# The quarter sums of the output weights on another engine, and two hand-dealt orders dealt anew

## The chip, the cores and the metric

The kernel runs on one core of a Trainium2 chip, in one launch. The core has five engines with instruction queues of their own: TensorE (PE in the profile; its weight loads are listed as PEld), VectorE (DVE), ScalarE (ACT), GpSimd (POOL) and SyncE (SP), which here only issues transfers. Each engine runs its queue in order. The metric is the device time of an execution in microseconds; the kernel before took 757.24 us, the median of three runs (756.76 to 757.77).

## The reference

```python
# attention: x (8, 8, 512, 64), state (8, 8, 32, 64): batch, heads, tokens or states, width
scores  = x @ state.T / 8;   a  = softmax(scores);   xread = a  @ state
scores2 = state @ x.T / 8;   a2 = softmax(scores2);  sread = a2 @ x
y = concatenate([xread, sread], axis=2)          # 544 rows for each batch and head
# bridge: (B, H, S, D) -> (B*S, H*D): 4352 rows of 512
# feed forward: d_model 512, d_ff 1536
xn  = y / sqrt(mean(y*y) + 1e-6) * rms_g
out = (silu(xn @ w_gate) * (xn @ w_val)) @ w_out     # (4352, 512) fp32
```

The three weight matrices arrive as 64-bit floats and are turned into fp32 in the kernel.

## The kernel before

**Batches.** The eight batches are worked one after the other, and then the 256 state rows of all batches together. For each batch the tokens' part of the attention is folded into the weights: the scores' softmax is aT_s, and own_weights (L702, copied by ACT at L714) multiplies the state into the gate and value weights, so that hidden_seven (L849) computes gate and value as v x aT_s. Batches 1 to 7 save products in the manner of Strassen and Winograd, seven for eight, with sums made on DVE and POOL: more_of_v (POOL, L729 to L732) and slot_sums (POOL, L767 to L770) for the inputs, L912 and L925 (DVE) to gather results, where L925 frees the PSUM bank of a pair of row blocks for the pair after next.

**The output product.** project_twice (L1152) applies the seven-product scheme twice. The outer seven products, counted o = 0 to 6, use seven outer blocks of the output weights, listed by outer_weights(): four blocks of wo and the three sums of them, kept in wt, which weight_sums (DVE, L995) makes once. Each outer product consists of seven inner ones; three of them need quarter sums of the outer block (w2) and three need quarter sums of h (h2, DVE, L1200 to L1206). quarter_sums of h are made anew in each batch. Those of the weights are made once, in batch 1, by weight_quarters: four differences of 128x384 fp32 for each of the seven outer blocks, the first three into a tile w2, the fourth in place; then w2 (576 KB) is written to DRAM (t2_d, t_d in the profile, L1108). From then on every batch fetches the seven sets back, one after the other, through a pool of three buffers (fetch_quarters, L1098). The same pool holds the w2 tiles while the sums are made, so a sum or a fetch waits until the tile three allocations earlier is free: written out, or read by the last product that uses it.

**The batch's own sums.** The results of the outer products are added by DVE (L1192) and combined by POOL (combine, L1180 to L1185), then stored by SP. Meanwhile the attention of the next batch is computed in pieces: scores (L356), softmax steps on DVE (L424 to L443), reading (L449), the row norm (DVE L393 and L396, PE L399, POOL L300, PE L307), and the states' part (L643).

**What sets the order.** The order of all five queues is written out by hand: each part of the work is a generator, and a string names which generator takes its next step. ORDER covers the first stretch: batch 0 (hidden, L745; project_as_ready, L952), the attention of batches 0 and 1, the conversion of the weights (exponents on ACT, L247 to L253; values on DVE, L274 to L283), and the start of batch 1. FIRST covers batch 1, PERIOD batches 2 to 6, LAST batch 7, STATES the state rows. Letters that matter here: z is one filler product (keep_awake, L1287), whose result nobody reads; k in ORDER is one step of weight_sums; w starts batch 1; S is the states' part of batch 1's attention; q in FIRST is one step of weight_quarters; G and g are fetches of quarter sets; f is a fetch of w; p, h, t, u are steps of the products and sums. A step that issues a transfer puts it on SP's queue at that place, and SP waits there until the transfer may start.

```python
streams.update(q=weight_quarters(), G=first_fetches_of_quarters())
...
for stream in FIRST if b == 1 else LAST if b + 1 == B else PERIOD:
    next(streams[stream])
```

Of the kernel before, what the change touches and what calls it, by code (L numbers as in the profile page):

```python
# [14 lines left out]
ALU = mybir.AluOpType  # L15
# [7 lines left out]
FLAT = 1793.0  # L23

ORDER = (
    "zzzzaaaadzzzababadeebebadzbzaddzabaeebeesabaszadbeazzzzdaaazbbbzzzszdsdzeezabazb"
    "AzeAbeddAbezedabazaAbbaavdbsbsvvdAAazdeazzzeAzhdstzdddehedAuehtddzhzddveevdpeuAd"
    "veAehdddepdAtdpddAdeeeAAhddehAtdAdApeevAuhspdvAesdveuAeeAdespdAsdddhdAdtepshduph"
    "eepAddvdephevtdevheAdduedASSpsthhededudAAepseeehdedAtAvsupdApeddvvdhAdAAddephdAh"
    "ApdedAtutdAdevdhdAdveAAeSvhutAhAhShpStdukSwwSwwkwwuwkppSkkppwSkkScpSSkcskkpSpwks"  # L30
    "Scck"
)

PERIOD = (
# [4 lines left out]
)  # L39

FIRST = (
    "htqhhqvtaaaxthuaqhuxqvvhatqhqtquhqaqhtquhqhxaqxquhtxfuhutqhthuhhqauthhthxuqquauq"
    "uqhxhaxtttuahhutxhvxhhGxaqkkukxuhkuhtthaqatqhuhauasGhthuqsGuuhuhtfttuahuhhgahlut"
    "huuuuftapaupsuhupupugkaappckppkpscpppkkqkpkkppkpkkppppfpakkakckppapkkkpkcapskppp"
    "acappaaapcsaapkaskakaakgkqpqpqpppkaksppaqkkgppapkpaakppaposakspokasckoosgagwswxo"
    "sxowpsxxcfsxlooxgf"
)
LAST = (
    "vxhhffththhtuhhhavuttuuhhtfuhhgxxthhhuuuxxtuthuhtthuhuxhutuvxxxvhthhutkxghhtuhut"
# [11 lines left out]
def kernel(  # L61
# [21 lines left out]
    VE, SE, GE, TE = nc.vector, nc.scalar, nc.gpsimd, nc.tensor  # L83
# [47 lines left out]
    def load_x(b, *queues):  # L131
# [6 lines left out]
        for c in range(NC):  # L138
# [12 lines left out]
                     in0=ones.to_broadcast([P, NC]), op=ALU.pow)  # L151
# [6 lines left out]
    for i in range(4):  # L158
        GE.tensor_copy(groups[:, i], ident[:, 0:Ns])
        for j in range(1, 4):  # L160
            GE.tensor_tensor(out=groups[:, i], in0=groups[:, i],
                             in1=ident[:, Ns * j:Ns * j + Ns], op=ALU.add)
# [336 lines left out]
    def second_half():  # L499

        yield from chunk_scores(1)
        yield from half_read(1)
# [260 lines left out]
    def slot_sums(b):  # L763

        tt = aT_t[b] = seven["late"].tile([P, 3, HS], F32, name="aT_t")
        b11, b12, b21, b22 = (aT_s[b][:, e, HS * i:HS * i + HS] for e in range(2) for i in range(2))
        GE.tensor_tensor(out=tt[:, 0], in0=b12, in1=b11, op=ALU.subtract)  # L767
        GE.tensor_tensor(out=tt[:, 1], in0=b22, in1=tt[:, 0], op=ALU.subtract)
        GE.tensor_tensor(out=tt[:, 2], in0=b21, in1=tt[:, 1], op=ALU.subtract)
        GE.tensor_tensor(out=b12, in0=b22, in1=b12, op=ALU.subtract)  # L770
# [14 lines left out]
    def tokens_of(b):  # L785

        return ([[aT_s[b][:, e, HS * i:HS * i + HS]] for e in range(2) for i in range(2)],
                [[aT_t[b][:, i]] for i in range(3)])
# [196 lines left out]
    def weight_sums():  # L985

        t1, t2, t4 = (seven["t"][:, i] for i in range(3))
        for k in range(0, HM, 2):
            def blk(i, j):
                return wo[:, HM * i + k:HM * i + k + 2, HD * j:HD * j + HD]  # L990
            for dst, a, b in ((t1[:, k:k + 2], blk(0, 1), blk(0, 0)),
                              (t2[:, k:k + 2], blk(1, 1), t1[:, k:k + 2]),
                              (blk(0, 1), blk(1, 1), blk(0, 1)),
                              (t4[:, k:k + 2], blk(1, 0), t2[:, k:k + 2])):
                VE.tensor_tensor(out=dst, in0=a, in1=b, op=ALU.subtract)  # L995
                yield
# [89 lines left out]
    def outer_weights():  # L1086

        t = seven["t"]

        def blk(i, j):  # L1090
            return wo[:, HM * i:HM * i + HM, HD * j:HD * j + HD]
        return [blk(0, 0), blk(1, 0), t[:, 1], t[:, 0], blk(0, 1), blk(1, 1), t[:, 2]]

    def fetch_quarters(n):

        if n < 7 * (B - 1):
            w2_sb[n] = seven["w2"].tile([P, 3, QM, QD], F32, name="w2")
            nc.sync.dma_start(out=w2_sb[n], in_=t2_d[n % 7])  # L1098

    def weight_quarters():  # L1100

        for o, (b11, b21, b12, b22) in enumerate(map(by_columns, outer_weights())):
            w2 = seven["w2"].tile([P, 3, QM, QD], F32, name="w2")
            for to, a, b in ((w2[:, 0], b12, b11), (w2[:, 1], b22, w2[:, 0]),
                             (w2[:, 2], b21, w2[:, 1]), (b12, b22, b12)):
                GE.tensor_tensor(out=to, in0=a, in1=b, op=ALU.subtract)  # L1106
                if to is b12:
                    nc.sync.dma_start(out=t2_d[o], in_=w2)  # L1108
                yield

    def by_columns(r):

        return [r[:, QM * i:QM * i + QM, QD * j:QD * j + QD] for j in range(2) for i in range(2)]
# [130 lines left out]
    def first_fetches_of_quarters():  # L1244

        for n in range(3):
            fetch_quarters(n)
            yield
# [25 lines left out]
    def of_batch_0(part):  # L1274

        for m in range(NM):
            if m not in parts_0:
                parts_0[m] = hidden(m, lambda e, k, m=m: v_sb[0, m // 2][0][:, e, m % 2, k, :],
                                    [aT_s[0][:, e, :] for e in range(2)])
            yield from parts_0[m][part]  # L1280

    def keep_awake():


        ps = fz.tile([P, 2, P], F32, name="f")
        while True:
            TE.matmul(out=ps, lhsT=ident, rhs=ident.unsqueeze(1).to_broadcast([P, 2, P]),  # L1287
                      start=True, stop=True)
            yield

    def first_of_batch(b):
        slot_sums(b)
        yield
        for mp in range(2):
            for part in own_weights(b, mp):
                yield from part
# [19 lines left out]
    for k in range(2, RAW_AHEAD):  # L1316
# [3 lines left out]
    streams = {"a": first_half(), "b": second_half(), "s": states_read(0), "A": tokens_read(1), "S": states_read(1),  # L1320
               "e": exponents(), "d": values(),
               "v": (step for mp in range(NM // 2) for part in own_weights(0, mp) for step in part),
               "h": of_batch_0(0), "t": of_batch_0(1), "u": of_batch_0(2),
               "p": project_as_ready(banks_0), "c": projected(banks_0, store_tokens(0)),
               "w": first_of_batch(1), "k": weight_sums(), "z": keep_awake()}
    by_hand = dict(engines={mybir.EngineType.PE, mybir.EngineType.DVE,
                            mybir.EngineType.Activation, mybir.EngineType.Pool,
                            mybir.EngineType.SP})
    with tc.manual_schedule(**by_hand):
        for stream in ORDER:  # L1330
            if stream in "ckw" and "s" not in seven:
                early.close()
                open_late()
            next(streams[stream])
        assert all(next(stream, done) is done for name, stream in streams.items() if name != "z")

        for b in range(1, B):
            h, t, u = hidden_seven(S, weights_of(b), lambda b=b: tokens_of(b), True)
            p, c, k, o = project_twice(b, store_tokens(b))
            own = [own_weights(b, mp) for mp in range(2, NM // 2)]  # L1340
            then = [own_weights(b + 1, mp) for mp in range(2)] if b + 1 < B else []
            streams = {"h": h, "t": t, "u": u, "p": p, "c": c, "k": k,
                       "v": (step for part in own for step in part[0]),
                       "x": (step for part in own + then for step in part[1])}
            streams.update(o=o, f=fetches(b), g=fetches_of_quarters(b))
            if b == 1:
                streams.update(q=weight_quarters(), G=first_fetches_of_quarters())
            if b + 1 < B:
                streams.update(l=loads(b + 2) if b + 2 < B else iter((0, 0)), a=tokens_read(b + 1), s=states_read(b + 1),
                               w=first_products(b + 1, then))  # L1350
            else:
                streams["a"] = (step for part in (state_norm(), sums_of_w([0])) for step in part)
            for stream in FIRST if b == 1 else LAST if b + 1 == B else PERIOD:
                next(streams[stream])
            assert all(next(stream, done) is done for stream in streams.values())
        n = B * (NM // 2)
        h, t, u = hidden_seven(NT, (state_weights, state_sums), state_tokens, True,
                               lambda mp: fetch(n + mp + W_BUFS))
        p, c, k = project_seven(NT, store_states, nc.scalar)
        list(weights_back())  # L1360
        streams = {"h": h, "t": t, "u": u, "p": p, "c": c, "k": k, "y": sums_of_w(range(1, NM // 2))}
        for stream in STATES:
            next(streams[stream])
        assert all(next(stream, done) is done for stream in streams.values())
# [29 lines left out]
```

## Time and profile before

| | |
|---|---|
| runs | 757.77, 757.24, 756.76 us |
| profiled execution, its own time | 756.69 us |
| its span, first to last instruction | 754.9 us |
| mean granted clock of TensorE | 0.998 |
| DRAM read, written | 116.46 MB, 28.77 MB |
| quarter sums on POOL (L1106) | 28, from 124.9 to 198.7 us |
| writes of the sets (L1108), fetches (L1098) | 7 and 49 of 576 KB |

Times within the profile are microseconds from the span's start. Busy times are those of one engine; a line number such as L1152 is the line of the kernel before. An fp32 product is listed as two passes, so the counts of matmul records are twice those of the instructions. In lists in order of time, the bracket behind a row says how long the engine had been idle before it and what ended that. The granted clock is the share of full speed that TensorE was given.

### The profile page before, as it was taken

How to read it: one execution, taken by the hardware profiler on the slowest of the kernel's cores; microseconds unless marked ns; L12 is line 12 of the kernel's file. 1: busy time of each engine (PE TensorE's matmuls, PEld its weight loads, DVE VectorE, ACT ScalarE, POOL GpSimd, SP SyncE). 2: the span in 40 equal slices, each digit the busy share in tenths (PEclk: the TensorE clock that was granted, in tenths of full speed). 3: DMA queues.
4: the chain of work that ended last, by engine and by line, in shares of the span. 5: the costliest groups of instructions: out<-in, count | busy, mean ns of one | idle time of the engine just before them, and what ended most of it. 6: DMA issues, size and time to landing. Idle time of an engine off the chain costs nothing.

```text
span 754.9 us, 14333 instructions
## 1 busy us (share of the span) xinstructions
PE 747.0 (99%) x5636; PEld 601.0 (80%) x5636; DVE 581.8 (77%) x982; ACT 350.2 (46%) x547; POOL 296.9 (39%) x387
## 2 busy tenths in 40 slices
PE   9999999999999999999999999999999999999998
PEld 7744444779868898879877997799788987899997
DVE  4897774789937996689858994799579965787952
ACT  6899863553244622653255415542456236411220
POOL 3000017971484227532565128312842275324600
PEclk9999999999999999999999999999999999999999
DMA  9998734934876077626673477527661855132411
GB/s 293 275 338 301 265 150 145 353 117 158 299 232 232 17 305 237 239 56 231 229 274 105 154 264 244 176 81 294 215 224 22 307 203 216 54 115 97 140 56 29
DMA packets 60995, 146.16 MB, mean 194 GB/s; under 512 B 14848, under 2 KB 31744, under 8 KB 54016
## 3 DMA queue, kind: packets, MB, share of 16 engines
q1 hardware_dynamic: 47808, 125.78, 47.1%
q10 hardware_dynamic: 13120, 19.47, 8.9%
q8 instruction: 45, 0.74, 0.4%
q14 instruction: 22, 0.18, 0.1%
HBM read 116.46 MB, written 28.77 MB: 192 GB/s over the span
## 4 chain that ended last, share of the span: by engine, by line
PE 96%; DMA 2%; DVE 1%; POOL 1%; issue 0%; ACT 0%; SPq 0%; POOLq 0%
PE f L849 39%; PE f L1152 29%; PE f L952 6%; PE pv L745 6%; PE at L702 3%; PE pv L702 3%; PE f L1015 2%; PE f L1287 2%; DMA t_d<-w 1%; PE at L643 1%; PE at L356 1%; DMA w<-t_d 1%; PE at L449 1%; PE pv L516 0%; PE at L307 0%; POOL w L1106 0%
## 5 line engine op out<-in xcount | busy, mean ns | idle before, releaser
L849 PE MATMUL f<-aT_s,v 128*128 128x256 f32 x504 | 119.6, 382 | 0.0
L849 PEld LDWEIGHTS f<-aT_s,v 128*128 128x128 f32 x504 | 94.5, 190 | 25.2 <-issue 11.4
L1180 POOL TENSOR_TENSOR kept<-kept 128x256 f32<-128x256 f32 x28 | 23.1, 826 | 189.7 <-DVE kept L1192 188.6
L1165 ACT COPY kept<-f 128x512 f32<-128x512 f32 (+1 forms) x56 | 29.7, 531 | 140.2 <-PE f L1152 98.4
L849 PE MATMUL f<-aT_t,vs 128*128 128x256 f32 x336 | 87.0, 382 | 0.0
L912 DVE TENSOR_TENSOR g<-g,f 128x512 f32<-128x512 f32 x84 | 57.4, 686 | 37.6 <-PE f L849 31.4
L1152 PE MATMUL f<-w,h 128*128 128x128 f32 x588 | 75.4, 278 | 0.0
L1152 PEld LDWEIGHTS f<-w,h 128*128 128x128 f32 x588 | 70.7, 194 | 4.9 <-issue 4.9
L849 PEld LDWEIGHTS f<-aT_t,vs 128*128 128x128 f32 x336 | 62.8, 190 | 14.0 <-POOL vs L729 3.7
L903 ACT ACTIVATE hb<-g 128x1024 f32<-128x1024 f32 x42 | 44.4, 1057 | 54.1 <-DVE g L912 54.1
L729 POOL TENSOR_TENSOR vs<-v 128x256 f32<-128x256 f32 x42 | 31.3, 745 | 80.7 <-ACT v L714 80.6
L300 POOL TENSOR_TENSOR ri<-ss,mhalf 128x4 f32<-128x4 f32 (+1 forms) x9 | 11.1, 1236 | 107.9 <-DVE s L603 78.6
L901 ACT COPY g<-f 128x512 f32<-128x512 f32 x42 | 24.6, 586 | 44.8 <-PE f L849 44.8
L952 PE MATMUL f<-wo,hb 128*128 128x512 f32 x96 | 45.2, 599 | 0.0
L745 PE MATMUL pv<-aT_s,v 128*128 128x512 f32 x96 | 44.4, 597 | 0.0
L849 PE MATMUL f<-aT_s,vs 128*128 128x256 f32 x168 | 43.6, 382 | 0.0
L849 PE MATMUL f<-aT_t,v 128*128 128x256 f32 x168 | 43.4, 381 | 0.0
L1152 PE MATMUL f<-wo,h 128*128 128x128 f32 x336 | 42.4, 276 | 0.0
L925 DVE TENSOR_TENSOR hb<-hb,f 128x512 f32<-128x512 f32 (+1 forms) x48 | 31.0, 647 | 14.8 <-PE f L849 14.8
L1152 PE MATMUL f<-wo,hb 128*128 128x128 f32 x336 | 42.1, 275 | 0.0
L912 DVE TENSOR_TENSOR c<-c,f 128x512 f32<-128x512 f32 (+1 forms) x48 | 31.3, 651 | 13.6 <-PE f L849 13.6
L925 DVE TENSOR_TENSOR hb<-hb,c 128x512 f32<-128x512 f32 (+1 forms) x48 | 36.7, 765 | 6.1 <-ACT hb L903 5.3
(225 smaller groups left out, 1680.7 us busy)
## 6 DMA issues: line engine op xcount, KB each, us to landing
w_m<-w_d SPq DMA_DIRECT2D x48, 1024.0 KB
w<-t_d SPq DMA_DIRECT2D x49, 576.0 KB
out_dram<-kept SPq DMA_DIRECT2D x28, 256.0 KB
raw<-in_moe_w_val_dram SPq DMA_DIRECT2D x6, 1024.0 KB
raw<-in_moe_w_out_dram SPq DMA_DIRECT2D x6, 1024.0 KB
w_d<-w_m SPq DMA_DIRECT2D x6, 1024.0 KB
x_b<-in_x_dram SPq DMA_DIRECT2D x6, 1024.0 KB
x_d<-xB ACTq DMA_DIRECT2D x6, 1024.0 KB
```

The costliest lines, as they stand in the source:

```text
L702: TE.matmul(out=pv[e][Ns * j:Ns * j + Ns, :], lhsT=stT_g[b][D * e:D * e + D, j, :], rhs=w[D * e:D * e + D, j].rearrange("p m k f -> p (m k ...
L729: GE.tensor_tensor(out=vs[:, 0], in0=a21, in1=a22, op=ALU.add)
L745: TE.matmul(out=to[0], lhsT=lhs(i, k), rhs=r, start=(i == 0), stop=(i == len(rhs) - 1))
L849: TE.matmul(out=ps[:, i, 0:half], lhsT=l[:, i, :], rhs=r, start=(start and i == 0 and k == 0), stop=(k == len(lhs) - 1), skip_group_check= ...
L901: SE.copy(gates(q)[1], q["x"][:, :, 0:half])
L903: SE.activation(out=hb[:, 2 * mp:2 * mp + 2, 0:n].rearrange("p m (c t) -> p m c t", c=2), in_=q["g"][:, :, :, 0:half], func=ACTF.Silu if s ...
L912: VE.tensor_tensor(out=to, in0=to, in1=q[ps][:, :, 0:half], op=ALU.add)
L925: VE.tensor_tensor(out=part, in0=part, in1=val, op=ALU.mult)
L952: TE.matmul(out=banks[r], lhsT=hb[:, m, P * r:P * r + P], rhs=wo[:, m, :], start=(m == 0), stop=(m == NM - 1))
L1152: TE.matmul(out=to[half][:, slot, :], lhsT=lhs[:, k, :], rhs=rhs[:, k, :], start=(fresh and n in (0, 4) and k == 0), stop=(k == QM - 1), s ...
L1165: SE.copy(of_half(k, i), banks[name][i])
L1180: GE.tensor_tensor(out=k[:, 4:8:3], in0=k[:, 5:6].to_broadcast([P, 2, QD]), in1=k[:, 4:8:3], op=ALU.add)
```

## The change

weight_quarters gets the engine and the list of outer blocks as arguments. The sums of blocks 2, 3 and 6, which are the three in wt, are made by VectorE at the end of the first stretch (twelve letters Q in ORDER); those of blocks 0, 1, 4 and 5, which lie in wo, are made by VectorE in batch 1 (sixteen q in FIRST, 28 before). GpSimd makes none. Each set is still written to DRAM by SP behind its fourth sum, and fetched as before, except that in the new FIRST the fetch of block 3 stands ahead of that of block 2. ORDER has 416 letters (404 before): the same letters and the twelve Q, in a new order. FIRST has 326 (338 before): the same letters and twelve q fewer, in a new order. PERIOD, LAST and STATES are untouched. From the inserted line on, line numbers are one higher.

```diff
 ORDER = (
-    "zzzzaaaadzzzababadeebebadzbzaddzabaeebeesabaszadbeazzzzdaaazbbbzzzszdsdzeezabazb"
...
-    "ApdedAtutdAdevdhdAdveAAeSvhutAhAhShpStdukSwwSwwkwwuwkppSkkppwSkkScpSSkcskkpSpwks"
-    "Scck"
+    "zzzzzzaaaaazzbbadedabdebezzaadazbbzezeaezbbsabadzzdbsbdzzabazabadszeeazbezdbbzza"
...
+    "dSdAeSAAhheApdAtAdASheuvAtvdevdhuhdShhSShtSwtkkuwuskSpkSkkpQpsppwkkkkpQpQQccQwpc"
+    "QQkkQQwwQwwSQQwc"
 )
...
 FIRST = (
-    "htqhhqvtaaaxthuaqhuxqvvhatqhqtquhqaqhtquhqhxaqxquhtxfuhutqhthuhhqauthhthxuqquauq"
...
-    "sxowpsxxcfsxlooxgf"
+    "vqahtaqaahhathhthhqxhuuuxthaqatvquvxthxqxqhtquhuuhhhutqhfqttuaaqxhhhtquqqaaxuhxh"
...
+    "cofxox"
 )
...
-    def weight_quarters():
-
-        for o, (b11, b21, b12, b22) in enumerate(map(by_columns, outer_weights())):
+    def weight_quarters(engine, *outer):
+
+        for o in outer:
+            b11, b21, b12, b22 = by_columns(outer_weights()[o])
             w2 = seven["w2"].tile([P, 3, QM, QD], F32, name="w2")
             for to, a, b in ((w2[:, 0], b12, b11), (w2[:, 1], b22, w2[:, 0]),
                              (w2[:, 2], b21, w2[:, 1]), (b12, b22, b12)):
-                GE.tensor_tensor(out=to, in0=a, in1=b, op=ALU.subtract)
+                engine.tensor_tensor(out=to, in0=a, in1=b, op=ALU.subtract)
                 if to is b12:
                     nc.sync.dma_start(out=t2_d[o], in_=w2)
                 yield
...
-               "w": first_of_batch(1), "k": weight_sums(), "z": keep_awake()}
+               "w": first_of_batch(1), "k": weight_sums(), "Q": weight_quarters(VE, 2, 3, 6), "z": keep_awake()}
...
-                streams.update(q=weight_quarters(), G=first_fetches_of_quarters())
+                streams.update(q=weight_quarters(VE, 0, 1, 4, 5), G=first_fetches_of_quarters())
```

## The prediction, made before the run

> **What bounds the kernel now.** I read the busy shares first, then who TensorE (PE) waits for, then the stretches, then the chain that ended last and the order of time around the one hole.
>
> ```profile
> PE 747.0 (99%) x5636; PEld 601.0 (80%) x5636; DVE 581.8 (77%) x982; ACT 350.2 (46%) x547; POOL 296.9 (39%) x387
> ...
> PE f L1287 <- POOL ident masks.py:199: 1.7, 1, 1.7
> PE f L1152 <- DMA w<-t_d: 1.1, 1, 1.1
> PE at L399 <- DVE part L396: 0.9, 1, 0.9
> PE f L849 <- DVE hb L925: 0.5, 1, 0.5
> ```
>
> PE is busy for 99% of the span and has four named waits. So the span is PE's work plus its holes, and the change adds or removes no matmul: both orders hold 34 filler matmuls (L1287) and the same products. All it can win lies in holes, and in what they do to PE's clock.
>
> ```profile
> 33.00:132.00 99.00, 99.00 (x502) 43.28 (x501) 74.14 (x100) 76.74 (x97) 16.86 (x20) 1.00 0.67 240
> 132.88:217.59 84.71, 82.65 (x670) 69.77 (x675) 71.30 (x119) 33.89 (x57) 50.47 (x54) 0.98 0.66 226
> 217.59:297.91 80.32, 80.32 (x671) 68.31 (x678) 65.02 (x116) 34.78 (x58) 35.11 (x47) 1.00 0.58 198
> 208.50:213.00 4.50, 4.49 (x25) 4.49 (x26) 2.11 (x5) 0.59 (x1) 3.80 (x5) 0.62 0.87 302
> ```
>
> Columns: stretch, its length, busy time of PE, weight load, VectorE (DVE), ScalarE (ACT) and GpSimd (POOL), granted PE clock, DMA share, GB/s. The first stretch has no hole from 33 to 132 us: nothing to win there. Batch 1 (second row) takes 84.71 us and batch 2, the same stream without quarter sums, 80.32: batch 1 loses 4.39. The last row is 4.5 us in which the clock was 0.62.
>
> ```profile
> 201.95 1.50 PE L1152 MATMUL f<-w,h 128*128 128x128 f32 x12
> 203.28 1.50 PE L1152 MATMUL f<-wo,h 128*128 128x128 f32 x12
> 204.62 1.50 PE L1152 MATMUL f<-wt,hb 128*128 128x128 f32 x12
> 207.00 0.36 PE L399 MATMUL at<-part,groups 128*128 128x16 f32 x2 [0.88 <-DVE part L396]
> 208.51 1.65 PE L1152 MATMUL f<-w,hb 128*128 128x128 f32 x6 [1.14 <-DMA w<-t_d]
> 209.95 2.45 PE L1152 MATMUL f<-w,h 128*128 128x128 f32 x12
> 212.24 0.83 PE L1152 MATMUL f<-wt,h 128*128 128x128 f32 x6
> ...
> 188.22 7.04 DMA t_d<-w
> 195.34 1.01 POOL w L1106
> 196.42 1.02 POOL w L1106
> 197.50 1.21 POOL w L1106
> 198.73 3.23 DMA t_d<-w
> 202.01 6.45 DMA w<-t_d
> ```
>
> The lower lines are the chain that ended last. POOL's sums of the seventh set wait for a buffer until set 5 has been written to DRAM (7.04), then are made, written (3.23) and fetched back (6.45); PE needs them at 208.5.
>
> **What is removed.** Waits: 0.88 + 1.14 = 2.02 us. Slow clock: the x6 and x12 after the hole take 1.44 and 2.29 from start to start (208.51, 209.95, 212.24), where the same shapes took 0.67 and 1.33 at 201.28 and 201.95: 0.77 + 0.96 = 1.73. Together 3.75. The clock row says the same: 4.5 x (1 - 0.62) = 1.71. Of the 4.39 the other 0.64 has no named cause, so the gain lies between 3.75 and 4.39; I take 3.75.
>
> Here a rule of the Trainium skill (TensorE: Matmul & The Clock Gate, "Why this matters for your kernels") reads otherwise: the clock falls only after idle gaps of over about 3 us. The row differs, since no gap here exceeds 1.14 and the granted clock behind it is 0.62. By the rule the removed wait would be worth 2.02 alone; the row decides.
>
> Both waits go. The DMA wait: in the changed order set 5, the last, is summed among the first four quarter sums of h (the first, L1200, began at 156.99), so by about 159 us, and all seven writes stand on SP's queue ahead of the first fetch; set 6 is needed at 208. The L396 wait: DVE stands one 384-element sum earlier (0.47) when it reaches L396, and DVE operations between 195 and 200 that POOL's sums stretched (L1204 0.81, L1206 1.35, L1200 1.35, against 0.55) fall back: 1.9. Together 2.4 against the 0.88.
>
> **What is added on DVE.** 28 sums of 128x384, off POOL. POOL took 1.0 to 1.3 each (medians by form). On DVE the same shape with two SBUF operands is L1200 to L1206: 0.55 busy, 0.47 apart when POOL is idle (183.37, 183.84), up to 1.34 beside POOL (156.99). I take 0.5, since with its sums POOL loses about half of its 50.5 us in batch 1 (24.4, added up over the rows of L1106 there); 1.34 is the upper end.
> Twelve stand at the end of the first stretch: 6 us. DVE waited 9.98 for L643 before 129.14. In the new order fourteen L952 (0.86 each) that stood ahead of L643 stand behind it, so it comes 12 us earlier, that room is used, and the weight sums L995 end before batch 1. On PE's path nothing.
> Sixteen stand in batch 1's L849 phase: 8 us. DVE's waits there, listed from 141.59 to 156.27, sum to 6.1, and the five L995 around its head (129.53 to 135.06: 6.4 busy) are done earlier. Queued behind them are L912 and L925, which free PE's banks: two sums (1.0) delay an L925 that ends at 150.9, whose bank PE takes again at about 153.5. Cover 2.6; price 0. Without it each late microsecond is PE's.
> By load, batch 1 on DVE is 65.02 + 16 x 0.5 = 73.0 of 80.3.
>
> **What is moved: DMAs and queues.** The three early writes (576 KB) stand on SP behind the load of batch 2's x, set 3's also behind three token stores, set 6's behind a w fetch that waits for an L702. Laying the new order along the starts of the same lines, set 2's is issued at about 124, set 3's at 131, set 6's at 133; they land in 3.2 to 7.0, and DVE reaches the sums that wait for them (sets 0, 1, 4) at 129, 141 and 148. Price 0. The fetches now go 0, 1, 3, 2: set 2's buffer comes free at 178.3, its first product stands at 185.7, so 7.4 against 3.2 to 6.5 for a transfer. Price 0, bounded under rivals.
>
> **The order dealt anew.** It can't gain (99.00 of 99.00); it can lose. I followed PE's order against ACT's and DVE's by the starts of the same lines. The tightest place: the fifth L745 needs the bank that silu L751 frees. In the new order twelve ACT steps and a table load lie between the copy L547 of the second half (about 23.6) and L751: starts of 1.06 to 1.30 for L247, L250, L253 and the load, 0.48 for copies, 12.8 in all, so 36.4, and PE comes at 36.1 to 36.5. Others have 0.1 to 0.6 to spare. Lower end 0, upper end one wait with its clock (1.14 + 1.73 = 2.9); I take 0.4, nearest to the places followed.
>
> **Sum.** 754.9 - 3.75 + 0.4 = 751.55 span; this execution took 756.69, so 1.79 lies around the span: 753.34. The median of the runs, 757.24, is 0.55 above it: **753.9**.
>
> **Rivals.**
> 1. *The new deal has a hole of its own* in the first stretch or batch 1, and the clock falls after it. For: ten places within 0.6, ACT busy 76.74 of 99. Against: the order before, as dense, has none there. 753.9 - 0.4 + 2.9 = 756.4: no change.
> 2. *DVE becomes the bound of batch 1: slower.* Place: the sixteen sums among L912 and L925 while POOL makes its v sums (L729 to L732). Price: (80.3 - 65.0) / 16 = 0.96 a sum fills DVE; from (84.71 - 65.0) / 16 = 1.23 on batch 1 is longer than before. At the 1.35 seen beside POOL: 65.0 + 21.6 = 86.6, 1.9 over before; with the 0.4: 759.5. For: DVE is already full from 160 to 189 (28.50 of 29), and L995 took up to 1.48 there. Against: POOL's work, which stretched them, is what leaves.
> The Trainium skill (GPSIMD Engine Reference, 1. Specifications) says that POOL's SBUF interface is shared with DVE, in contention with DVE instructions of two SBUF inputs, as these sums are. By that rule, the trace agrees (0.55 and 1.34).
> 3. *The third fetch is late.* From about 159 on a write, three fetches of sets and three of w (5.5 MB) are issued at once; at 318 GB/s, the rate of 132 to 160, they drain by 176, just before 178.3. If the queue is 2 us behind: a wait of 2 + 6.5 - 7.4 = 1.1 and its 1.73 of clock: 753.9 + 2.8 = 756.7, no change.
> 4. *The slow clock is not the wait's.* The rule above holds, and the 0.62 had another cause that stays: 753.9 + 1.73 = 755.6.
> That the change doesn't do what it says I leave out: no quarter sum stands on POOL in the new order.
>
> **Chances.** Forecast 0.64 (own range 752.6 to 755.7), rivals 0.12, 0.13, 0.07, 0.04. A measurement of this kernel can tell about 0.2% (1.5 us) from no change: 755.7 and 758.8. Faster: 0.64 + 0.04 and 0.02 of rival 1's milder ends, 0.70. Same: 0.10 + 0.07 = 0.17. Slower: 0.13. The low end is 757.24 - 4.39 less 0.2 of scatter, 752.6; the high end reaches past rivals 1 and 3 to 758.3, and leaves rival 2 out.
>
> **What would show it.** Right: batch 1 near 80.7, no PE wait on w<-t_d or part, clock 1.00 throughout, sums at 0.5 to 0.6 on DVE, POOL some 30 us less busy, first L849 at 132.9 to 133.5. Wrong: filler followed by a named wait before 133; L849 or L1152 waiting for L912 or L925 with sums near 1.3 (rival 2); a wait on w<-t_d near 185 (rival 3); waits gone and a stretch below 1.00 left (rival 4).

## The result and the profile after

The changed kernel takes 753.22 us (median of 8 runs, 752.47 to 754.70); the kernel before, run on the same chip beside it, 756.90 us (8 runs, 754.51 to 758.33). The ratio is 0.996, 95% interval 0.9943 to 0.9976: 3.7 us or 0.5% faster. The profiled execution has a span of 751.2 us and took 752.98.

First the busy shares on the page of the changed kernel, then its answer on whom TensorE waits for (columns: engine and line, releaser, us in total, times, longest).

```profile
PE 744.2 (99%) x5636; PEld 598.3 (80%) x5636; DVE 589.4 (78%) x1010; ACT 352.9 (47%) x549; POOL 265.8 (35%) x359
```

```profile
PE f L1288 <- POOL ident masks.py:199: 1.7, 1, 1.7
PE f L849 <- DVE hb L925: 0.5, 1, 0.5
```

The waits on w<-t_d and on part are gone; the wait at the start and the 0.5 among the state rows are those of before. GpSimd (POOL) is 31 us less busy, VectorE (DVE) only 8 more: the 28 sums are 16.41 us of its busy time, and its other work takes 8.8 us less now that GpSimd makes none of the sums. TensorE's (PE's) busy time fell by 2.8 us although it does the same products: part of its busy time had been work at a slow clock.

Where the time came from shows when both kernels are cut at like instructions, the first L849 of batches 1, 2 and 3. Rows of the changed kernel, then of the kernel before; columns as in the prediction.

```profile
33.00:133.38 100.38, 100.38 (x516) 42.66 (x515) 81.67 (x116) 76.32 (x97) 8.09 (x9) 1.00 0.69 251
133.38:213.63 80.25, 80.25 (x662) 67.86 (x662) 72.27 (x130) 36.28 (x60) 29.82 (x38) 1.00 0.69 233
213.63:293.79 80.16, 80.16 (x670) 68.21 (x663) 64.95 (x115) 35.52 (x60) 35.10 (x47) 1.00 0.57 195
```

```profile
132.71:218.54 85.83, 83.77 (x679) 70.05 (x677) 71.76 (x120) 34.58 (x58) 51.59 (x56) 0.98 0.66 228
218.54:298.70 80.16, 80.16 (x670) 68.20 (x662) 64.73 (x115) 34.78 (x58) 34.87 (x47) 1.00 0.58 198
```

Batch 1 now takes 80.25 us, within 0.1 of batch 2: almost nothing is lost in it. Before it took 85.83, in which stood one block of 16 L702 and one product of L318 (0.89 and 0.11 from start to start) that the changed kernel runs ahead of its first L849. So batch 1 gave 85.83 - 1.00 - 80.25 = 4.58 us. The first stretch ends at 133.38 with these products, 132.38 without them, against 132.71: 0.33 less. From the first L849 of batch 2 to the last product both take the same (530.01 us before, 529.96 after). The last product starts 4.96 us earlier (743.59 against 748.55), and the span is only 3.7 shorter. The rest is in the last rows in order of time, of the changed kernel and of the kernel before (start, duration, engine, line):

```profile
743.59 2.75 PE L1015 MATMUL f<-wt,hb 128*128 128x256 f32 x12
...
746.78 2.19 ACTq L1271 DMA_DIRECT2D out_dram<-h  x2
```

```profile
748.55 2.75 PE L1015 MATMUL f<-wt,hb 128*128 128x256 f32 x12
...
751.75 0.85 ACTq L1270 DMA_DIRECT2D out_dram<-h  x2
```

From the start of that product to the end of the span 6.35 us pass before and 7.61 after: the last two stores were issued in 2.19 us instead of 0.85. That is chance, not the change: in the twelve profiles of the experiments it is 6.3 to 6.5 in eight and 7.3 to 8.3 in four, and kernels built on the changed one and on the one before are in both groups.

The place of the old hole, in order of time, in the changed kernel:

```profile
204.00 0.83 PE L1153 MATMUL f<-wt,hb 128*128 128x128 f32 x6
204.67 0.29 PE L399 MATMUL at<-part,groups 128*128 128x16 f32 x2
204.81 0.92 PE L1153 MATMUL f<-wt,hb 128*128 128x128 f32 x6
205.56 0.83 PE L1153 MATMUL f<-w,hb 128*128 128x128 f32 x6
206.23 1.50 PE L1153 MATMUL f<-w,h 128*128 128x128 f32 x12
207.57 0.83 PE L1153 MATMUL f<-wt,h 128*128 128x128 f32 x6
```

No row carries a wait, and the starts are 0.67 apart for x6 and 1.34 for x12; the one L399 product costs 0.22 (x6, L399 and x6 take 1.56 from 204.00 to 205.56). And the sums themselves (durations in ns, least, median, most; first and last start):

```profile
L1107 DVE TENSOR_TENSOR w<-wo,w x8: 546/559/1019, 133.8 to 156.9; 128x384 f32<-128x384 f32 x8
L1107 DVE TENSOR_TENSOR w<-wt,w x6: 547/557/557, 122.3 to 128.4; 128x384 f32<-128x384 f32 x6
L1107 DVE TENSOR_TENSOR w<-wo x4: 551/816/1083, 129.4 to 150.8; 128x384 f32<-128x384 f32 x4
L1107 DVE TENSOR_TENSOR wo<-wo x4: 515/550/552, 140.1 to 157.8; 128x384 f32<-128x384 f32 x4
```

The last one starts at 157.8; GpSimd's last had started at 198.7. A sum takes 0.55; three of the 28, beside GpSimd's work, take 1.02 to 1.08.

### The profile page after: what moved, and what is told of

The parts are those of the page before. It is cut to its first block, busy times and chain, and to the rows that moved or that the text cites. A ratio compares the mean times of both kernels' runs of the same rounds, so it can differ in the third digit from the quotient of the medians.

```text
span 751.2 us, 14331 instructions
## 1 busy us (share of the span) xinstructions
PE 744.2 (99%) x5636; PEld 598.3 (80%) x5636; DVE 589.4 (78%) x1010; ACT 352.9 (47%) x549; POOL 265.8 (35%) x359
## 4 chain that ended last, share of the span: by engine, by line
PE 98%; DVE 1%; issue 0%; POOL 0%; ACT 0%; POOLq 0%
PE f L849 39%; PE f L1153 31%; PE pv L745 6%; PE f L952 6%; PE at L702 3%; PE pv L702 3%; PE f L1015 2%; PE f L1288 2%; PE at L643 1%; PE at L356 1%; PE at L449 1%; PE at L307 0%; PE pv L516 0%; PE at L329 0%; PE at L617 0%; PE at L511 0%
## 5 line engine op out<-in xcount | busy, mean ns | idle before, releaser
L849 PE MATMUL f<-aT_s,v 128*128 128x256 f32 x504 | 119.3, 382 | 0.0
L849 PEld LDWEIGHTS f<-aT_s,v 128*128 128x128 f32 x504 | 94.7, 190 | 23.2 <-issue 9.2
L849 PE MATMUL f<-aT_t,vs 128*128 128x256 f32 x336 | 87.0, 383 | 0.0
L912 DVE TENSOR_TENSOR g<-g,f 128x512 f32<-128x512 f32 x84 | 57.3, 686 | 36.3 <-PE f L849 25.2
L849 PEld LDWEIGHTS f<-aT_t,vs 128*128 128x128 f32 x336 | 62.7, 190 | 14.6 <-POOL vs L729 3.4
L729 POOL TENSOR_TENSOR vs<-v 128x256 f32<-128x256 f32 x42 | 31.4, 747 | 102.9 <-ACT v L714 102.8
L849 PE MATMUL f<-aT_s,vs 128*128 128x256 f32 x168 | 43.7, 383 | 0.0
L849 PE MATMUL f<-aT_t,v 128*128 128x256 f32 x168 | 43.4, 381 | 0.0
L925 DVE TENSOR_TENSOR hb<-hb,f 128x512 f32<-128x512 f32 (+1 forms) x48 | 31.0, 646 | 13.3 <-PE f L849 13.3
L1153 PEld LDWEIGHTS f<-wo,hb 128*128 128x128 f32 x336 | 40.4, 192 | 1.2 <-issue 0.8
L925 DVE TENSOR_TENSOR hb<-hb,c 128x512 f32<-128x512 f32 (+1 forms) x48 | 36.2, 754 | 5.9 <-ACT hb L903 5.1
```

The lines of the kernel that those rows point to most:

```text
L729: GE.tensor_tensor(out=vs[:, 0], in0=a21, in1=a22, op=ALU.add)
L849: TE.matmul(out=ps[:, i, 0:half], lhsT=l[:, i, :], rhs=r, start=(start and i == 0 and k == 0), stop=(k == len(lhs) - 1), skip_group_check= ...
L912: VE.tensor_tensor(out=to, in0=to, in1=q[ps][:, :, 0:half], op=ALU.add)
L925: VE.tensor_tensor(out=part, in0=part, in1=val, op=ALU.mult)
L1153: TE.matmul(out=to[half][:, slot, :], lhsT=lhs[:, k, :], rhs=rhs[:, k, :], start=(fresh and n in (0, 4) and k == 0), stop=(k == QM - 1), s ...
```

## The experiments

Three theories. The hole: the gain is the hole ahead of batch 1's last outer product, and it closes once the seventh set is written early. The engine: GpSimd's relief is what pays. The deal: the new order is what pays. "Before" is the kernel before on the same chip beside the run.

| run | median us | before | ratio, 95% interval |
|---|---|---|---|
| changed kernel | 753.22 | 756.90 | 0.996 (0.9943 to 0.9976) |
| e1 engine alone | 764.59 | 757.49 | 1.0119 (1.0086 to 1.0152) |
| e2 deal alone, sums on GpSimd | 757.73 | 757.49 | 1.0016 (0.9996 to 1.0035) |
| e4 old order of batch 1 | 763.56 | 757.49 | 1.0095 (1.0066 to 1.0124) |
| e5 old order of the first stretch | 760.29 | 757.49 | 1.0041 (1.0020 to 1.0061) |
| e6 hole filled, in the kernel before | 755.94 | 755.86 | 1.0007 (0.9988 to 1.0026) |
| e7 four sums more | 754.14 | 755.86 | 0.9985 (0.9970 to 1.0000) |
| e8 twelve sums more | 761.38 | 755.86 | 1.0084 (1.0060 to 1.0108) |
| e9 = e4, xG asked for together | 763.36 | 757.04 | 1.0097 (1.0065 to 1.0130) |
| e10 first three sets on GpSimd | 753.93 | 757.04 | 0.9966 (0.9950 to 0.9983) |
| e11 = e4, fetches held back | 757.07 | 755.42 | 1.0015 (0.9996 to 1.0035) |
| b1, b2: the kernel before again | 757.42, 753.97 | 757.04 | one execution each |

### The engine alone (e1)

```diff
-                GE.tensor_tensor(out=to, in0=a, in1=b, op=ALU.subtract)
+                VE.tensor_tensor(out=to, in0=a, in1=b, op=ALU.subtract)
```

> The kernel before with its 28 quarter sums on VectorE instead of GpSimd, every letter of the orders where it was. Theory (the gain is the hole before batch 1's last outer product, and it closes only when the seventh set is summed and written early): the letters of sets 5 and 6 stay late in the order, so the seventh set is still written at about 195 us and fetched back by about 207; the hole at 206 to 212 stays, and VectorE has 28 x 0.55 = 15.4 us more in batch 1 beside 71.3, 86.7 of 85.7, so PE waits for it as well: 0 to 6 us slower than before. Rival (taking the sums off GpSimd is what pays): no wait on the fetched set, 3 to 5 us faster than before.

7.1 us slower, more than the 0 to 6 expected. TensorE in order of time at the hole:

```profile
212.11 0.37 PE L399 MATMUL at<-part,groups 128*128 128x16 f32 x2 [2.33 <-DVE part L396]
214.68 1.31 PE L1152 MATMUL f<-w,hb 128*128 128x128 f32 x6 [2.20 <-DMA w<-t_d]
215.78 2.77 PE L1152 MATMUL f<-w,h 128*128 128x128 f32 x12
```

Both waits stay and have grown, from 0.88 and 1.14 to 2.33 and 2.20, and TensorE waits another 2.3 us in batch 1 for L912 and L925. The faster engine doesn't bring the last sum earlier, since its letter stands late in the order: it starts at 208.3, on GpSimd it had started at 198.7. So the engine alone gains nothing. What rival 2 of the prediction describes, TensorE held up by a late VectorE, this kernel shows, though VectorE is busy for only 80.26 of the 91.99 us that batch 1 takes.

### The deal alone (e2)

```diff
-               "Q": weight_quarters(VE, 2, 3, 6),
+               "Q": weight_quarters(GE, 2, 3, 6),
...
-                streams.update(q=weight_quarters(VE, 0, 1, 4, 5), ...)
+                streams.update(q=weight_quarters(GE, 0, 1, 4, 5), ...)
```

> The changed kernel with all 28 quarter sums back on GpSimd, at the new places: three sets at the end of the first stretch, four in batch 1. Theory: the last set is written about 165 us instead of 198, so the hole at 206 to 212 is gone whichever engine adds: at least 2 of the 3.7 us stay. What it may lose is GpSimd's time: 16 sums of 1.1 us are 17.6 us on a queue that also makes the v sums of L849, up to 2 us of PE waiting for those. So 1.5 to 4 us faster than before. Rival (the engine pays): GpSimd is as loaded per set as before, within 1 us of the kernel before.

No change against before: less than the 1.5 to 4 us that I expected of the hole. The hole at 206 to 212 is indeed gone, and a new one stands at 155. Its row in order of time, and the stretches around it (POOL's busy time is the fifth pair, the granted clock follows it):

```profile
157.27 0.91 PE L849 MATMUL f<-aT_t,vs 128*128 128x256 f32 x3 [2.14 <-POOL vs L729]
```

```profile
155.00:157.27 2.27, 0.13 (x1) 0.00 (x1) 1.38 (x1) 0.80 (x2) 2.14 (x3) 1.00 1.07 348
157.27:158.00 0.73, 0.73 (x3) 0.68 (x4) 0.00 (x0) 0.00 (x0) 0.70 (x2) 1.00 1.00 362
158.00:161.50 3.50, 3.50 (x10) 2.63 (x8) 1.13 (x2) 0.58 (x1) 3.42 (x6) 0.51 0.94 341
```

GpSimd makes the sixteen sums at 1.0 us each ahead of the v sums (L729) that L849 reads: 2.14 of wait, then 3.5 us at half clock. Batch 1 takes 84.84. The deal alone moves the hole; in batch 1 the engine is needed too.

### Where the engine matters (e10)

```diff
-               "Q": weight_quarters(VE, 2, 3, 6),
+               "Q": weight_quarters(GE, 2, 3, 6),
```

> The changed kernel with the first three sets (twelve sums at the end of the first stretch) on GpSimd, the four of batch 1 on VectorE. Theory (the engine matters only where its own work feeds PE: e2's wait was for v sums in batch 1): GpSimd has 92 of 100 us free in the first stretch, 12 x 1.0 us fit; in e2 they ended at 138.4, some 9 us later than on VectorE, so that GpSimd's first v sums of batch 1 come later; within 1 us of the changed kernel, and VectorE has 6.6 us less. Rival (any sum on GpSimd late in the first stretch holds PE): a wait on vs (L729) early in batch 1, 2 to 4 us slower than the changed kernel.

Within 0.1% of the changed kernel, no new wait of TensorE, batch 1 80.58. For the three early sets either engine does; beside e2 this shows that it is the sixteen sums of batch 1 that must leave GpSimd.

### The two orders (e4, e5)

e4 keeps the old FIRST, with the last twelve q taken out; e5 keeps the old ORDER, with QQQQQQQQQQQQ behind its end.

> The changed kernel with the new order of the first stretch, but the old order of batch 1, of which the last twelve letters q are taken out (sets 0, 1, 4 and 5 take the first sixteen). VectorE makes the sums. Theory: the hole is gone, since the last of the sixteen is the 75th letter (about 155 us): 3 to 5 us of it are won; the old order leaves no room on VectorE for 8.8 us of sums, so up to 2 us are lost to banks that L912 and L925 free late: 1.5 to 4 us faster than before. Rival (the new deal of batch 1 is what pays): no gain, within 1 us of before, or slower.

> The changed kernel with the new order of batch 1, but the old order of the first stretch, with the twelve letters Q behind its end. VectorE makes the sums. Theory: the hole of batch 1 is gone (about 4.7 us), but the twelve sums, 6.6 us, now stand behind the last L995 and ahead of batch 1's first L912: VectorE comes some 6.6 us late to it, of which some 2.6 us are covered, so PE waits some 4 us for banks early in batch 1: within 1.5 us of the kernel before. Rival (VectorE has enough room there): as fast as the changed kernel, 3 to 4 us faster than before.

e5 came out worse than expected, e4 far worse. e5's wait is the expected one, L849 on L912 at 144.47, but it is 4.7 us long and costs 7.1 (batch 1 takes 87.35). The stretches of the wait and behind it show why:

```profile
139.50:144.47 4.97, 0.29 (x2) 0.03 (x1) 4.97 (x9) 0.00 (x0) 2.57 (x3) 0.77 0.26 108
144.47:149.00 4.53, 4.53 (x16) 2.72 (x24) 4.50 (x9) 2.13 (x3) 0.00 (x0) 0.50 0.74 292
```

DVE is full while PE stands, and PE then runs 4.5 us at 0.50. Only one place of the twelve sums was tried in the old order, that behind its end. In e4 the old hole is gone, but PE waits at a place that nobody had named. In order of time on TensorE:

```profile
164.67 1.04 PE L356 MATMUL at<-xG,stT 64*32 64x512 f32 x2
169.87 1.96 PE L356 MATMUL at<-xG,stT 64*32 64x512 f32 x14 [4.16 <-DMA xG<-x_d]
```

The scores of batch 2 wait for the last quarter of xG. ScalarE issued it at 159.25; the chain of waits gives it 10.48 us. Three fetches of quarter sets had been issued close together at 153.8, 154.2 and 158.1, and a fetch of w (1024 KB) at 158.5, all on SyncE's queue. In the kernel before the three went at 146.1, 156.8 and 178.5 and that fetch of w at 178.9; now the last write is issued at 153.3 (198.7 before), and the fetches follow it. e9 and e11 try whether they made xG late.

### Why the old order of batch 1 loses (e9, e11)

e9 moves three letters a in e4's FIRST, so that all four quarters of xG are issued together; e11 holds the fetches back.

```diff
-    "...quhqhxaqxquhtxfuhutqhthuhhqauthhthxuquauuhxhaxtttuahhutxhvxhhGxakk..."
+    "...quhqhxaqxquhtxfuhutqhthuhhqaaaauthhthxuquuuhxhxtttuhhutxhvxhhGxakk..."
```

> The old order of batch 1 with sixteen q (the kernel of e4), with three letters a moved ahead (77th, 83rd, 89th to behind the 66th), so that ScalarE issues the last three quarters of the load xG<-x_d right behind the first, at about 152, ahead of the three fetches of quarter sets that SyncE issues from 153.8. Theory (e4 lost to xG standing behind fetches that the earlier sums had let go): the wait of 4.2 us at L356 is gone with its clock, 7 to 8 us faster than e4, about 755.5 to 757 us; some 3 us for late L912 and L925 stay. Rival (the old order's late VectorE would hold PE at the same place anyway): less than 3 us faster than e4.

Missed: the same time as e4. The wait at L356 is gone, but another took its place, as ScalarE's waits show:

```profile
ACT hb L903 <- DVE g L912: 6.5, 2, 3.3
ACT c L899 <- DMA xG<-x_d: 4.7, 1, 4.7
```

By the chain of waits the issue of the fourth quarter waited for the first to land, which took 5.7 us (151.8 to 157.5). ScalarE stood behind it, its copy L899 came late, and PE waited 3.8 us for that bank. So e9 doesn't decide whether the fetches had made xG late.

```diff
             w2_sb[n] = seven["w2"].tile([P, 3, QM, QD], F32, name="w2")
+            if n < 3:
+                VE.memset(w2_sb[n][:, 0, 0, 0:1], 0.0)
...
-    "...utxhvxhhGxakkukx..."
+    "...utxhvxhhxaGkkukx..."
```

> The old order of batch 1 with sixteen q (the kernel of e4), with the first three fetches of quarter sets held back: a write of one element per partition by VectorE into each buffer, at the letter G, stands ahead of the fetch, so that SyncE can't issue it before VectorE comes there, and the first G stands behind the scores of batch 2. So the three fetches are issued after about 160 us instead of 153.8 to 158.4, behind the last quarter of xG<-x_d (159.3). Theory (in e4 xG stood behind the fetches that the earlier sums had let go): the wait at L356 falls from 4.2 to below 1.5 us, its slow clock goes, and the kernel is 5 to 8 us faster than e4, about 756 to 758.5. Rival (xG is late because ScalarE issues it late, or for other transfers): the wait at L356 stays above 3 us and the time within 1.5 us of e4.

As the theory has it: 6.5 us below e4's median, and in the profiles TensorE gains 7.5 us between L356 and the products behind it. With the fetches issued from 160.3, PE in order of time:

```profile
164.12 1.09 PE L356 MATMUL at<-xG,stT 64*32 64x512 f32 x16
165.14 1.13 PE L849 MATMUL f<-aT_s,v 128*128 128x256 f32 x4
```

No wait, though xG's last quarter was issued at the same place (158.7). So the early transfers of SyncE's queue were what made it late. Which of them is not shown: holding the three fetches back also held back the fetch of w behind them (from 158.5 in e4 to 170.1). The new deal of batch 1 asks for xG at 148.8 to 151.5, ahead of its fetches (from 157.9). e11 still has L849 waiting in batch 1, 1.8 us for L912 and L925 and 0.4 for ScalarE's L896, and loses 2.8 us to the kernel before up to 200 us, then wins 4.0 at the old hole. That sums up the old order with sixteen sums on DVE: some 4 won, 2.8 lost, mostly to late banks, and 7.5 lost where the transfers meet.

### How much room VectorE has left (e7, e8)

```diff
                 engine.tensor_tensor(out=to, in0=a, in1=b, op=ALU.subtract)
+                if o in (0, 1, 4, 5) and a is b12:
+                    engine.tensor_tensor(out=to, in0=a, in1=b, op=ALU.subtract)
```

e8 has `to is not b12` in place of `a is b12`.

> The changed kernel with the first sum of each of the four sets of batch 1 made twice: four more sums of 0.55, 2.2 us more on VectorE. Theory (cover of about 2.6 us was left): no wait of PE, within 0.6 us of the changed kernel. Rival (VectorE is already the bound in the stretch of L849): 2.2 us slower than the changed kernel.

> The changed kernel with the first three sums of each of the four sets of batch 1 made twice: twelve more sums of 0.55, 6.6 us more on VectorE. Theory (cover of about 2.6 us was left): PE waits for about 4 us at banks that L912 and L925 free, 3 to 6 us slower than the changed kernel with the clock. Rival (by load: 72.3 + 6.6 = 78.9 us of 80.3 fit): within 1 us of the changed kernel.

Both lose more than expected. Four sums (2.2 us) lengthen batch 1 from 80.25 to 81.40, with one wait of 0.48 at L849 on L912: by the batch's length about half of them is covered. Its median is 0.9 us above the changed kernel's in another set of runs, 1.9 by the ratios, whose intervals just meet. Twelve (6.6 us) lengthen batch 1 to 88.81: waits of 0.72 on L925 at 148, 0.23 on L925 and 3.02 on L912 between 154 and 159, together the 4 us expected, and then PE's clock is 0.50 from 158.18 to 165.01, twice as long as behind the hole. That slow stretch, of which PE is idle for 0.71, costs (6.83 - 0.71) / 2 = 3.06 by my estimate, and 8.56 - 3.06 = 5.5 are left of lateness. So 1.1 us of sums are covered by the batch's length in both kernels (2.2 - 1.15 and 6.6 - 5.5); by the named waits alone it would be 1.7 and 2.6. VectorE's load was reckoned at 78.9 of 80.3 us and measured at 80.36.

### The clock behind the hole (e6, b1, b2)

In e6 fillers stand in the kernel before ahead of and behind L399:

```diff
+        fill(2, 0)
         TE.matmul(out=sp, lhsT=groups..., rhs=part, start=True, stop=True)
+        fill(3, 1)
```

> The kernel before with filler products in its hole: two ahead of L399 (2 x 0.44 us) and three behind it, into a PSUM bank of which nobody reads that part, so that TensorE is not idle between 206.1 and 208.5. The wait for the fetched set itself stays. Theory (the slow clock after the hole comes of PE's idle time): the granted clock stays at 1.00 in 208 to 213, and the execution is 1.73 us faster than before, 1.4 to 2.0 with L307's chain. Rival (the slow clock has another cause): the clock falls to about 0.5 there as before, and the time is within 0.4 us of before.

> The kernel before, unchanged, for one more profile. Its executions spread over 7 us (752.9 to 760.2), the changed kernel's over 2.2. Theory (the spread is the hole: the fetched set comes early or late by chance of the transfers): the waits at L399 and on w<-t_d and the slow clock behind them differ from the first profile's 2.02 and 1.7 us by about as much as the execution's time differs from 756.7; an execution below 755 shows no clock below 0.9 at 206 to 213. Rival (the spread is the start and the last stores): the same hole of about 4.7 us whatever the time.

> The same once more, with the same two expectations: by the theory the hole follows the execution's time, by the rival it is about 4.7 us again.

The clock changes only at the ends of stretches of 3.413 us (the last section has the figures). Here are those around the hole, of e6, then b1, then b2, then the first profile of before; the first pair is the length and PE's busy time, and the difference is PE's idle time:

```profile
205.98:209.39 3.41, 3.16 (x19) 2.57 (x18) 2.25 (x6) 0.00 (x0) 1.39 (x2) 1.00 0.90 298
209.39:212.81 3.42, 3.42 (x87) 3.25 (x86) 3.33 (x8) 0.59 (x1) 2.96 (x4) 1.00 0.90 319
```

```profile
206.64:210.05 3.41, 1.01 (x7) 0.94 (x8) 3.33 (x10) 0.00 (x0) 2.33 (x3) 1.00 0.85 299
210.05:213.47 3.42, 3.42 (x18) 3.42 (x17) 1.11 (x4) 0.59 (x1) 2.79 (x5) 0.50 0.86 248
```

```profile
203.13:206.55 3.42, 2.49 (x22) 2.23 (x20) 3.42 (x7) 0.00 (x0) 3.10 (x4) 1.00 0.87 268
206.55:209.96 3.41, 2.59 (x23) 2.60 (x24) 3.11 (x10) 0.59 (x1) 2.42 (x3) 1.00 1.15 371
```

```profile
205.10:208.52 3.42, 1.41 (x13) 1.15 (x11) 3.35 (x10) 0.00 (x0) 2.26 (x4) 1.00 0.78 274
208.52:211.93 3.41, 3.41 (x16) 3.41 (x17) 2.09 (x5) 0.41 (x1) 3.25 (x5) 0.50 0.91 302
```

With the hole filled the clock stays at 1.00, and the products behind it run 1.7 us faster (offset against the kernel before +0.16 at 208.5, -1.56 at 212.2): the slow clock came of the idle time. But the median did not fall, as my theory had it. b1 and b2 tell why. The hole differs from one execution to the next: idle for 2.70 us (1.21 + 1.49) in b1, 2.02 in the first profile, 1.74 in b2, divided over two stretches, and there the clock does not fall at all. b1 took 757.42 us, b2 753.97.

The runs on record bear this out, since each has its mean granted clock. Of the 75 executions of the kernel before that ran beside the experiments, 39 had a clock of 0.999 or 1.000 and a median of 754.64 us (36 of them under 756), and 36 had 0.995 to 0.998 and a median of 757.59 (none under 756). By these figures the kernel before pays for a slow clock in about half of its executions; over all it ranged from 752.90 to 760.18. The changed kernel's eight have 0.999 or 1.000. In e6 eleven of twelve runs have such a clock and lie within 754.83 to 756.21, where the 14 of the kernel before beside them with such a clock have a median of 754.56. So e6 saves the slow clock where it would fall, and pays some 1.4 us for the fillers in every execution. Its batch 1 says the same: 84.75 us, against 83.74 in b2 and 85.83 in the first profile.

## Why the prediction was right, point by point

**The bound and the hole.** Right. PE's order is full, both named waits are gone, the clock is 1.00 throughout batch 1, and batch 1 takes what batch 2 takes, but for 0.1.

**The sum.** 751.55 of span predicted, 751.2 measured; 753.9 against 753.22. The total is nearer than its terms:

| term | predicted | profile |
|---|---|---|
| waits and slow clock in batch 1 | -3.75, at most -4.39 | -4.58 |
| first stretch dealt anew | +0.4 | -0.33 |
| from batch 2 to the last product | 0 | -0.05 |
| last stores | 0 | +1.26 |
| span | -3.35 | -3.7 |

"Together 3.75" was mis-sized. The waits of 0.88 and 1.14 are idle times up to modelled ends. From start to start the last x12, L399 and its wait take 3.89 us (204.62 to 208.51), and as much work takes 1.56 in the changed kernel: 2.33 lost instead of 2.02. Two small places had no name: 0.31 at L1152 at 198.29 and 0.15 at 216.35. With the 1.73 of clock that is 4.52 of the 4.58. The upper end of 4.39 was short because my two windows were not cut at like instructions.

The 0.33 of the first stretch is no gain of the deal. The first L516 starts at 8.03 us, 0.55 earlier than before, and by that place profiles of the same order on PE differ anyway (7.67 to 9.30). From there to batch 1 pass 124.35 us without the moved products (124.32 to 124.37 in e2, e7, e8 and e10), before 124.13 (124.13 to 124.15 in e1, b1 and b2). So the new deal costs 0.2 there, the sign and half the size of the 0.4 that I took. The last stores' 1.26 came by chance and hid most of the two misses of 0.83 and 0.73.

There is luck in the price of the hole as well. I took it from one execution. With the moved products left out, batch 1 loses 4.58 us in that one, 2.49 in b2 and 6.25 in b1, so the same reading of b2 would have forecast a gain of some 2 us less. The forecast of the time itself hangs on that less, since the hole that is taken off is that of the profile it starts from. The gain does: 3.7 us is a mean over executions of the kernel before that lost a slow clock and others that did not.

**The clock step.** Right, and shown by e6. The Trainium skill (TensorE: Matmul & The Clock Gate, "Part 1: The HAM clock gate (the "warmup" mystery)") gives the half clock and a window of about 3.4 us; the traces agree on both (0.50, for 3.41 or twice 3.41 us). It lets the clock fall after an idle window, and the section cited in the prediction after gaps of over about 3 us. Here a stretch of 3.41 us that was idle for 2.01 in two pieces did it, and one that was idle for 1.89 did not: the row decided rightly, and rival 4 falls. What I did not see is that the 1.73 is on a threshold: one profile gave a fixed price to something that about half of the executions do not pay.

**The sums on VectorE.** Their time (0.5, measured 0.55) and the load (73.0, measured 72.27) were right, price 0 as well. "Cover 2.6" was not: by the batch's length e7 and e8 show 1.1, and 2.6 only by e8's named waits. Rival 2 was nearer than its numbers said. Its threshold of 0.96 us a sum was made by load over the whole batch; e8, with 80.36 us of load, takes 88.81 for batch 1, since the sums stand in the one stretch where L912 and L925 feed PE's banks.

**The engine.** I had argued for the move off GpSimd only from what its sums do to VectorE's times. e2 shows the part I had left out: on GpSimd, at the new places, the sums hold up its own L729.

**"The order dealt anew. It can't gain."** True of PE's holes, and it misled. The deal is no source of gain but a condition: without the new FIRST the kernel is 10.3 us slower than with it (e4 against the changed kernel, medians of two sets of runs), without the new ORDER, the twelve sums behind its end, 7.1. I looked at xG nowhere. The writes of the early sets came as forecast, at 123.6, 130.8 and 133.4 (about 124, 131 and 133). I wrote of transfers that drain in time for the third fetch, and they do (no wait near 185, rival 3 falls); the transfer that early fetches endanger is another one, on another queue.

## What to carry to other kernels

Moving work off the engine that is late helps only together with an earlier place in the order, and an earlier end lets transfers go earlier: ask which load on another queue is then behind them. Cost a hole from start to start between like instructions, in several profiles, before a term of it is trusted: here it was 1.7 to 2.7 us idle, with or without 1.7 us of slow clock behind it. Where a kernel's executions fall into two groups, see which of them the profile is from: their mean granted clock tells. Room on an engine is what one stretch leaves between the operations that others wait for, not the batch's load.

## What the hardware did that I had not expected

TensorE's clock goes by stretches of 3.413 us that do not start with the idle time. In all fourteen profiles every fall and rise lies a whole number of such stretches behind the first rise: in the kernel before the first rise is at 7.13, the fall at 208.52 and the next rise at 211.93, 59 and 60 of them later. In these profiles PE's idle time within one stretch (by modelled ends) parts the falls from the rest:

| profile | idle in the stretch ahead of the fall | idle in the first slow one | slow for |
|---|---|---|---|
| before, e2, b1, e1 | 2.01, 2.14, 2.40, 2.64 | 0.00 in each | 3.41 |
| e4, e8, e5, e9 | 2.26, 2.31, 2.39, 2.86 | 1.90, 0.71, 2.29, 0.92 | 6.83 |

In batch 1 the clock stayed at full speed behind a stretch that was idle for 1.89 (e1, 208.25 to 211.67), and in b2 behind 0.93 and 0.82. So the fall comes at the end of a stretch, not of the wait: 0.65 us after PE had resumed in b1 and 0.81 in e2, at once in the kernel before. The first rise is at 4.6 to 7.9 us in the fourteen profiles, so a hole can lie in one stretch in one execution and in two in the next. A wait of 2.14 us in one stretch cost 4.59 (e2, batch 1), b2's 1.74 in two cost 2.49. Why the clock came back after one stretch in four profiles and after two in the others is not tested; the table shows only that PE was idle again in the first slow stretch of the latter.

A load of 256 KB took 10.5 us beside three fetches of 576 KB and one of 1024 KB, issued up to 5.5 us ahead of it on another queue (e4); with those held back it landed within 5.4 (e11, issued at 158.7, read at 164.12 without a wait).
